# Channel attention with a gated MLP: six of eight f groups in seven products, two sums of each by transfers

## Chip, cores and metric

One Trainium2 chip, one core. The metric is the time of one execution on the device in microseconds; the median of three runs stands for a kernel.

## The reference

Four batches of channel attention (a softmax over a 256 x 256 matrix), whose result goes through a two-layer MLP with a squared gate. All in float32.

```python
def _attn_ref(q, k, v, tau) -> np.ndarray:          # q, k, v: 4 x 6080 x 256
    qn = q / (np.linalg.norm(q, axis=1, keepdims=True) + 1e-06)
    kn = k / (np.linalg.norm(k, axis=1, keepdims=True) + 1e-06)
    s = kn.transpose(0, 2, 1) @ qn / tau
    s = s - s.max(-1, keepdims=True)
    a = np.exp(s)
    a /= a.sum(-1, keepdims=True) + 1e-09
    return (v @ a).astype(np.float32)

def _moe_ref(x, w_in, w_out) -> np.ndarray:          # x: 24320 x 256, d_ff 2048
    h = x @ w_in
    beta = 1.0
    neg = h <= -beta
    pos = h >= beta
    g = np.where(pos, h, np.where(neg, 0.0, (h + beta) ** 2 / (4.0 * beta)))
    return (g @ w_out).astype(np.float32)
```

## The kernel before

**What is computed on TensorE.** For each batch the 256 x 256 attention matrix is multiplied into `w_in` once (`make_W`, `make_W2`); the result is stored in DRAM and loaded again for each use (`load_W`, an SP transfer of 896 KB). After that a batch is two large products: h = v W and out = g `w_out`. Every float32 value is split into a high half, rounded for TensorE's fast format, and a low half, the difference. A product is three matmuls: high by high, high by low, low by high (`mm3`, line 651). A product on 496 columns is now and then done on 512 (`width`, line 98).

**Tiling.** A batch's 6080 tokens are six pairs of token blocks, of 512 columns in the first four pairs and 496 in the last two. The 2048 columns of f are eight groups of 256 (i = 0 to 7). A group is one batch b, pair k and i, 192 in all, numbered g. In each group h is a 2 x 2 block product, and `h_ops` does it in the seven products of Strassen's method in Winograd's form: 21 matmuls in place of 24. The gate follows on ScalarE and VectorE (`saturate`, `square`, `clamp`), then the halves (`halves_of`: the high half a copy on ScalarE or VectorE, line 994 or 995, the low half a subtraction on VectorE, line 996).

**The second product.** `o_ops` does a plain group: eight products of three matmuls, on four banks of PSUM (`O00` to `O11`) that add up over the eight groups of a pair. `o_forms` does a group in the seven-product form. For it, sums of the four blocks of g are needed: `left` and `right` are two buffers with two blocks each, and `plus` (line 1059, its instruction at 1061) adds block to block on VectorE, three times in a group, while `added` (1080, its instruction at 1082) adds the fourth sum by a transfer between SBUF tiles, issued from GpSimd. Sums of the blocks of `w_out` (`S1` to `S4`) are made once by `make_forms` and stay in `wsum`. Groups in this form go in stacks, `STACKS = ((0,1),(4,5,6))`: within a pair, groups 0 and 1, then 4, 5 and 6. A stack's first two products are done group by group; the other five only when its last group is there, with copies and two sums of banks between them (lines 1101 to 1121: S2, then `add`, then S3, then `add`, then the last three). Before a stack begins and at the end of a pair the banks are emptied (`ends`): a ScalarE copy (line 1173), and a store, by SP, or by GpSimd with accumulation in DRAM for the pair's second half. The first pair has no stack; the last has `LAST = ((0,1),)`. So 22 pairs of five groups and one of two are in the form: 112 groups.

**What sets the order.** The whole program is written first as a list of operations with their reads and writes (`od.op`); `ORDER` is a table with the number of the next operation at each place, and `place` puts the operations in that order and gives each its buffers: 22 blocks (`NB`), 12 small ones (`NH`), 4 large ones for pairs of halves (`NX`), 3 for W (`NW`). Each engine, SP's and GpSimd's queue too, works its part off in order, and waits where an operand or a buffer isn't free. Numbers such as `T_FORM`, `due` and `pad` are used where the table is made; in the finished program the table decides.

## Time and profile before

| | before |
|---|---|
| median of three runs | 2098.42 us (2096.66 to 2106.02) |
| profiled execution, its own time | 2101.45 us |
| its span | 2099.5 us |
| TensorE busy | 2081.7 us, 9593 matmuls |
| VectorE busy | 2020.1 us |
| ScalarE busy | 1902.4 us |
| GpSimd busy | 265.0 us |
| DMA | 422.27 MB, mean 201 GB/s |

Busy time is the time in which at least one instruction of an engine is under way; consecutive instructions overlap a little, so an instruction's own duration is longer than the pace at which a row of them goes. The span runs from the first to the last instruction of the profiled execution. A transfer has two times: its issue on the engine whose queue it is in, and its landing.

### The profile page before, as it was taken

How to read it: one execution, taken by the hardware profiler on the slowest of the kernel's cores; microseconds unless marked ns; L12 is line 12 of the kernel's file. 1: busy time of each engine (PE TensorE's matmuls, PEld its weight loads, DVE VectorE, ACT ScalarE, POOL GpSimd, SP SyncE). 2: the span in 40 equal slices, each digit the busy share in tenths (PEclk: the TensorE clock that was granted, in tenths of full speed). 3: DMA queues.
4: the chain of work that ended last, by engine and by line, in shares of the span. 5: the costliest groups of instructions: out<-in, count | busy, mean ns of one | idle time of the engine just before them, and what ended most of it. 6: DMA issues, size and time to landing. Idle time of an engine off the chain costs nothing. (4 is left out here: it accounts for less than half of the span.)

```text
span 2099.5 us, 28487 instructions
## 1 busy us (share of the span) xinstructions
PE 2081.7 (99%) x9593; PEld 1741.5 (83%) x9593; DVE 2020.1 (96%) x3162; ACT 1902.4 (91%) x3111; POOL 265.0 (13%) x304
## 2 busy tenths in 40 slices
PE   9999999999999999999999999999999999999999
PEld 8888878888888888888788888888888888888887
DVE  7999999999999999999999999999999999999996
ACT  6899999999899999998899999989999999888884
POOL 0000011121101111111111120110111211111100
PEclk9999999999999999999999999999999999999999
DMA  9756667886668686785866887776786766566652
GB/s 381 283 206 201 214 173 228 227 236 163 162 215 264 175 251 201 214 256 140 204 171 205 253 212 245 207 197 200 194 214 180 169 184 162 148 176 170 164 132 69
DMA packets 133619, 422.27 MB, mean 201 GB/s; under 512 B 15202, under 2 KB 37346, under 8 KB 131170
## 3 DMA queue, kind: packets, MB, share of 16 engines
q1 hardware_dynamic: 91426, 344.70, 47.4%
q0 software_dynamic: 42048, 75.77, 22.8%
q8 instruction: 75, 1.23, 0.2%
q14 instruction: 70, 0.57, 0.1%
HBM read 310.05 MB, written 81.30 MB: 186 GB/s over the span
## 5 line engine op out<-in xcount | busy, mean ns | idle before, releaser
L654 PE MATMUL bank<-blk,w_mem 128*128 128x512 f32 (+1 forms) x4032 | 1038.3, 389 | 9.2 <-ACT bank L1016 5.4
L654 PEld LDWEIGHTS bank<-blk,w_mem 128*128 128x128 f32 x4032 | 749.9, 188 | 167.7 <-ACT bank L1016 8.9
L654 PE MATMUL bank<-x,wout 128*128 128x512 f32 (+1 forms) x2595 | 665.8, 387 | 1.6 <-DVE x L996 1.6
L654 PEld LDWEIGHTS bank<-x,wout 128*128 128x128 f32 x2595 | 485.7, 188 | 98.7 <-DVE x L996 2.4
L996 DVE TENSOR_TENSOR x<-blk,x 128x1024 fp32r<-128x1024 f32 (+1 forms) x384 | 459.9, 1210 | 6.4 <-ACT x L994 5.5
L978 ACT ACTIVATE blk<-blk 128x512 f32<-128x512 f32 (+3 forms) x576 | 438.0, 772 | 7.3
L983 DVE SCALAR_TENSOR_TENSOR blk<-bank,blk 128x512 f32<-128x512 f32 (+1 forms) x576 | 387.8, 681 | 15.3 <-ACT blk L978 14.1
L973 ACT ACTIVATE blk<-bank 128x512 f32<-128x512 f32 (+1 forms) x576 | 337.6, 593 | 46.7 <-PE bank L654 43.3
L994 ACT CAST x<-blk 128x1024 fp32r<-128x1024 f32 (+1 forms) x331 | 340.5, 1041 | 25.6 <-PE bank L654 10.4
L996 DVE TENSOR_TENSOR blk<-blk,blk 128x512 fp32r<-128x512 f32 (+1 forms) x336 | 226.7, 682 | 1.6
L1082 POOL DMA_DIRECT2D blk<-blk x112 | 98.5, 889 | 967.9 <-DVE blk L996 407.8
L654 PE MATMUL bank<-blk,wsum 128*128 128x512 f32 (+1 forms) x672 | 178.3, 387 | 0.0
L654 PE MATMUL bank<-x,wsum 128*128 128x512 f32 (+1 forms) x672 | 173.1, 388 | 0.0
L919 POOL DMA_DIRECT2D half<-vT x92 | 93.0, 1044 | 590.0 <-DVE blk L883 321.2
L994 ACT CAST blk<-blk 128x512 fp32r<-128x512 f32 (+1 forms) x242 | 148.3, 616 | 11.6 <-DVE blk L1061 8.9
L1061 DVE TENSOR_TENSOR blk<-blk,blk 128x512 f32<-128x512 f32 (+1 forms) x224 | 152.2, 682 | 1.8
L654 PEld LDWEIGHTS bank<-x,wsum 128*128 128x128 f32 x672 | 125.7, 188 | 25.8 <-DVE bank L1102 0.6
L654 PEld LDWEIGHTS bank<-blk,wsum 128*128 128x128 f32 x672 | 125.7, 188 | 24.9
L1019 DVE SCALAR_TENSOR_TENSOR bank<-bank,half 128x512 f32<-128x512 f32 (+1 forms) x192 | 132.7, 691 | 8.5 <-PE bank L654 2.4
L1023 DVE SCALAR_TENSOR_TENSOR half<-bank,half 128x512 f32<-128x512 f32 (+1 forms) x192 | 130.9, 682 | 5.5 <-PE bank L654 4.4
L654 PE MATMUL bank<-blk,blk 128*128 128x256 f32 (+2 forms) x704 | 135.4, 305 | 0.0
L973 ACT ACTIVATE blk<-half 128x512 f32<-128x512 f32 (+1 forms) x192 | 120.7, 629 | 11.8 <-DVE half L1023 10.2
(99 smaller groups left out, 2127.1 us busy)
## 6 DMA issues: line engine op xcount, KB each, us to landing
w_mem<-w_d SPq DMA_DIRECT2D x160, 896.0 KB, 6.0
blk<-kqT SPq DMA_DIRECT2D x60, 512.0 KB, 7.1
w_d<-w_mem SPq DMA_DIRECT2D x32, 896.0 KB, 7.8
blk<-kq SPq DMA_DIRECT2D x55, 512.0 KB, 6.2
half<-vT SPq DMA_DIRECT2D x75, 256.0 KB, 5.3
blk<-blk POOLq DMA_DIRECT2D x75, 256.0 KB, 5.2
kq<-kq SPq DMA_DIRECT2D x18, 1024.0 KB, 9.1
outT<-half SPq DMA_DIRECT2D x64, 256.0 KB, 6.1
```

The source lines that it names most:

```text
L654: nc.tensor.matmul(out, lhsT=lhs(a), rhs=rhs(c), start=start and m == 0, stop=stop and m == 2, skip_group_check=skip)
L919: op("POOL", POOL_DMA, lambda: nc.gpsimd.dma_start(out=tt(x), in_=blk(j, h), accum_op=ALU.add), w=[ts[x]], due=due + d, gates=gates, size= ...
L973: op("ACT", act_ps(n) if psum else act_us(n), lambda: nc.scalar.activation(pb.ap[:, j, :n], src(), AF.Relu, bias=0.5, scale=0.5), r=[h, pb ...
L978: op("ACT", act_us(len(us) * n), lambda: nc.scalar.activation(at(), at(), AF.Square), r=[pb], w=us, due=due, tag=(53, due - G * (due // G)))
L983: op("DVE", dve_us(n), lambda: nc.vector.scalar_tensor_tensor(out=us(), in0=src(), scalar=1.0, in1=us(), op0=ALU.max, op1=ALU.min), r=[h, ...
L994: op("ACT", act_us(m * n), lambda: nc.scalar.copy(half_(0), src()), r=r, w=[t], due=d_hi, other=("DVE", dve1_us(m * n), lambda: nc.vector. ...
L996: op("DVE", dve_us(m * n), lambda: nc.vector.tensor_tensor(out=half_(1), in0=src(), in1=f32(half_(0)), op=ALU.subtract), r=r, w=[t], due=d ...
L1019: op("DVE", dve_us(n), lambda: nc.vector.scalar_tensor_tensor(out=bb.ap[:, :n], in0=z.ap[:, :n], scalar=-1.0, in1=m5.ap[:, :n], op0=ALU.mu ...
L1023: op("DVE", dve_us(n), lambda: nc.vector.scalar_tensor_tensor(out=h22.ap[:, :n], in0=z.ap[:, :n], scalar=-1.0, in1=m5.ap[:, :n], op0=ALU.m ...
L1061: op("DVE", dve_us(n), lambda: V.tensor_tensor(out=at(out), in0=at(a), in1=at(c), op=ALU.add), r=[b for p, j in (a, c) for b in (p[0], p[1 ...
L1082: op("POOL", POOL_DMA, lambda: nc.gpsimd.dma_start(out=at(out), in_=at(a), accum_op=ALU.add), r=[a[0][0], a[0][1 + a[1]], out[0][0]], w=[o ...
```

## The change

`STACKS` and `LAST` both become `((0,1,2),(4,5,6))`, so six groups of every pair but the first are in the seven-product form, 138 in all; groups 3 and 7 stay plain. The sum of `right`'s two blocks is made by `added` in place of `plus`, so a group has two transfers and two VectorE sums. One more set of forms (i = 2) is made. The form `S4` goes into the place of `w_out`'s block (x = 0, ct = 1), which a group in the seven-product form doesn't read, once the first pair, whose groups are plain, has read it; `wsum` has three forms in place of four, and there is one more small buffer (`NH` 13). In the last pair the first half's results are copied to SBUF and kept there (`kept`), and VectorE adds the second half's to them before the store; before, that pair's banks were emptied at its end alone. `ORDER` is a new table.

```diff
--- before.py
+++ after.py
@@ -251,7 +251,7 @@
 G = 16
 U = 32
 NB = 22
-NH = 12
+NH = 13
 NX = 4
 NW = 3
 
@@ -269,153 +269,160 @@
 T_SO = 2.7
 T_P4 = -5.7
 ORDER = (
-    "c-n2c4@`3XmnU{P&mD%PH;ls?>pIpLYmIS@wT30cI4mVBWhrG@$6*M=I)pMTVW~?ULRd<yF|2hgF@!jdYh2c$gdv7yD9iF=UBXh<CDyu*wZ^*E"
...
+    "c-mdM4NQ7}mnU{P-ao^`bBD(gV~lGYW2`mCSmUzRSi&00G7LjmhVZZ~!!is*DPycP##m#GHP%?;IK;S?Sk@BCQii$=!$TQ{r7TMb!??y8*BWDt"
...
 )
-STACKS = ((0,1),(4,5,6))
-LAST = ((0,1),)
-FORMED = (0,1,4,5,6)
+STACKS = ((0,1,2),(4,5,6))
+LAST = ((0,1,2),(4,5,6))
+FORMED = (0,1,4,2,5,6)
 STARTUP = (
     ('v', 0, -463.4, 13),
     ('out', 0, -426.7, 16),
@@ -534,7 +541,7 @@
     kq_early = Pool(kq_mem, kq_all)
     pools["g"].held[:4] = [kq_all] * 4
     for i in FORMED:
-        pools[f"wsum{i}"] = Pool([sb(f"wsum{i}", [2, 4, P], F32R)])
+        pools[f"wsum{i}"] = Pool([sb(f"wsum{i}", [2, 3, P], F32R)])
     win_dram = [dram.tile([P, 2 * WIN], U32, name=f"win_d{i}") for i in range(FP // 2)]
     row_dram = [dram.tile([CT, P], F32, name=f"row_d{b}") for b in range(B)]
     w_dram = [[dram.tile([P, WSZ], U32, name=f"w_d{b}_{i}") for i in range(FP)] for b in range(B)]
@@ -596,12 +603,13 @@
         convert(w_out[i].rearrange("p a f -> p (a f)"), wout_buf[i], lambda: wout_buf[i].ap, due, gates)
 
     form_buf = {i: buf(f"wsum{i}") for i in FORMED}
-    FORMS = (S1, S2, S3, S4)
+    FORMS = (S1, S2, S3)
+    a21_buf = {i: Buf(ap=wout[:, i]) for i in FORMED}
 
     def wform(i, s, a):
         if s in FORMS:
             return form_buf[i].ap[:, a, FORMS.index(s), :]
-        x, ct = {A11: (0, 0), A12: (1, 0), A22: (1, 1)}[s]
+        x, ct = {A11: (0, 0), S4: (0, 1), A12: (1, 0), A22: (1, 1)}[s]
         return wout[:, i, a, x, ct * P:(ct + 1) * P]
 
     def make_forms(i, due, step=0.4):
@@ -612,13 +620,19 @@
         op("DVE", dve_us(512), lambda: nc.vector.tensor_tensor(out=w_ap(), in0=flat(0), in1=flat(1), op=ALU.add),
            r=[wout_buf[i], pb], w=[w], due=due, tag=11)
         at = {A11: 0, A21: 1, A12: 2, A22: 3}
-        forms(lambda x: f_ap()[:, FORMS.index(x) * P:(FORMS.index(x) + 1) * P],
+        forms(lambda x: f_ap()[:, (S1, S2, S3, S4).index(x) * P:][:, :P],
               lambda x: w_ap()[:, at[x] * P:(at[x] + 1) * P], [w, pb], f, due + step)
         fl = lambda a: to.ap[:, a].rearrange("p j f -> p (j f)")
-        op("ACT", act_us(512), lambda: nc.scalar.copy(fl(0), f_ap()), r=[f, pb], w=[to],
+        late = lambda a: wout[:, i, a, 0, P:2 * P]
+        part, last = (lambda: f_ap()[:, :3 * P]), (lambda: f_ap()[:, 3 * P:])
+        op("ACT", act_us(384), lambda: nc.scalar.copy(fl(0), part()), r=[f, pb], w=[to],
            due=due + 2 * step, tag=12)
-        op("DVE", dve_us(512), lambda: nc.vector.tensor_tensor(out=fl(1), in0=f_ap(), in1=fl(0).bitcast(F32),
+        op("DVE", dve_us(384), lambda: nc.vector.tensor_tensor(out=fl(1), in0=part(), in1=fl(0).bitcast(F32),
                                                               op=ALU.subtract), r=[f, pb], w=[to], due=due + 3 * step, tag=13)
+        op("ACT", act_us(128), lambda: nc.scalar.copy(late(0), last()), r=[f, pb], w=[a21_buf[i]],
+           due=due + 2 * step, tag=12)
+        op("DVE", dve_us(128), lambda: nc.vector.tensor_tensor(out=late(1), in0=last(), in1=late(0).bitcast(F32),
+                                                              op=ALU.subtract), r=[f, pb], w=[a21_buf[i]], due=due + 3 * step, tag=13)
 
     def forms(out, src, r, w, due):
 
@@ -946,7 +960,7 @@
     NG = len(groups)
     mark = [None] * (NG + 8)
     o_buf, out_buf = {}, {}
-    gt, gu = {}, {}
+    gt, gu, kept = {}, {}, {}
 
     def stack_of(g):
 
@@ -1075,18 +1089,18 @@
                 m = od.width(n, TB, j in (V_T3, V_22, V_T4, V_21))
                 mm3(out.ap[:, :m], lambda a: wform(x, s, a), lambda c: at(c, m), start, False)
 
-            op("PE", mm_us(n), fn, r=[t, wout_buf[x], form_buf[x]], w=[out], due=due, tag=(63, s))
+            op("PE", mm_us(n), fn, r=[t, wout_buf[x], form_buf[x], a21_buf[x]], w=[out], due=due, tag=(63, s))
 
         def added(out, a, c, due):
             at = lambda x: x[0][0].ap[:, x[1], :n]
             op("POOL", POOL_DMA, lambda: nc.gpsimd.dma_start(out=at(out), in_=at(a), accum_op=ALU.add),
-               r=[a[0][0], a[0][1 + a[1]], out[0][0]], w=[out[0][1 + out[1]]], due=due - 8, size=n * 512, tag=(62, "d"))
+               r=[a[0][0], a[0][1 + a[1]], out[0][0]], w=[out[0][1 + out[1]]], due=due - 8, size=n * 512, pad=3.0, tag=(62, "d"))
 
         f = d + T_FORM
         halves(left, (V_11,), f + 18, 0)
         plus((left, 0), (right, 0), (left, 0), f + 18.5)
         halves(left, (V_T1,), f + 19, 1)
-        plus((right, 0), (right, 1), (right, 0), f + 20.5)
+        added((right, 0), (right, 1), (right, 0), f + 20.5)
         plus((left, 0), (right, 1), (left, 0), f + 20)
         halves(left, (V_T2,), f + 20.5, 2)
         halves(right, (V_T3, V_22), f + 22, 1)
@@ -1133,11 +1147,11 @@
                 o = o_buf[b, k, y, ct]
                 c0 = b * N + t0 + y * n
 
-                def store(yb, m0, m1, due, ct=ct, c0=c0):
+                def store(yb, m0, m1, due, w=None, ct=ct, c0=c0):
                     to = outT[ct * P:(ct + 1) * P, c0 + m0:c0 + m1]
                     if g < FP or g >= NG - FP or i < STACKS[1][0]:
                         out_buf[c0, ct] = Buf(ap=outT)
-                        op("SP", 0.45, lambda: nc.sync.dma_start(out=to, in_=yb.ap[:, :m1 - m0]), r=[yb],
+                        op("SP", 0.45, lambda: nc.sync.dma_start(out=to, in_=yb.ap[:, m0 if w else 0:m1 if w else m1 - m0]), r=[yb, *([w] if w else ())],
                            w=[out_buf[c0, ct]], due=due, size=(m1 - m0) * 512, tag=67)
                     else:
                         op("POOL", POOL_DMA, lambda: nc.gpsimd.dma_start(out=to, in_=yb.ap[:, :m1 - m0], accum_op=ALU.add),
@@ -1152,27 +1166,38 @@
                         mm3(o.ap[:, :m], lambda a: wout[:, i, a, x, ct * P:(ct + 1) * P], lambda c: at(c, m),
                             g == 0 and x == 0, ends(g) and (x == 1 or end))
 
-                    op("PE", mm_us(n), fn, r=[t, wout_buf[i]], w=[o], due=d + T_O + dues[2 * ct + x], tag=(69, y, x, ct))
+                    op("PE", mm_us(n), fn, r=[t, wout_buf[i], *([a21_buf[i]] if i in FORMED and (x, ct) == (0, 1) else ())], w=[o], due=d + T_O + dues[2 * ct + x], tag=(69, y, x, ct))
                 due = d + dues[2 * ct + 1] + 3
                 if end:
 
                     (t, at), m = gt[g, 1, y], n // 2
                     for m0, m1, bank in ((0, m, "A"), (m, n, "B")):
-                        yb, q = buf("y"), buf(bank)
-                        op("ACT", act_us(m1 - m0), lambda yb=yb, m0=m0, m1=m1: nc.scalar.copy(
-                            yb.ap[:, :m1 - m0], o.ap[:, m0:m1]), r=[o], w=[yb], due=due, tag=70)
+                        (yb, ws), q = kept[y, ct], buf(bank)
+                        w = ws[m0 > 0]
+                        op("DVE", dve_us(m1 - m0), lambda yb=yb, m0=m0, m1=m1: nc.vector.tensor_tensor(
+                            out=yb.ap[:, m0:m1], in0=o.ap[:, m0:m1], in1=yb.ap[:, m0:m1], op=ALU.add), r=[o, yb], w=[w],
+                           due=due, psum=True, tag=70)
                         op("PE", mm_us(m1 - m0), lambda q=q, m0=m0, m1=m1: mm3(
                             q.ap[:, :m1 - m0], lambda a: wout[:, i, a, 1, ct * P:(ct + 1) * P],
                             lambda c: at(c, n)[:, m0:m1], True, True), r=[t, wout_buf[i]], w=[q], due=due, tag=71)
-                        op("DVE", dve_us(m1 - m0), lambda yb=yb, q=q, m=m1 - m0: nc.vector.tensor_tensor(
-                            out=yb.ap[:, :m], in0=q.ap[:, :m], in1=yb.ap[:, :m], op=ALU.add), r=[q], w=[yb],
+                        op("DVE", dve_us(m1 - m0), lambda yb=yb, q=q, m0=m0, m1=m1: nc.vector.tensor_tensor(
+                            out=yb.ap[:, m0:m1], in0=q.ap[:, :m1 - m0], in1=yb.ap[:, m0:m1], op=ALU.add), r=[q, yb], w=[w],
                            due=due + 1, psum=True, tag=72)
-                        store(yb, m0, m1, due + 1)
+                        store(yb, m0, m1, due + 1, w)
+                elif g == len(groups) - 1:
+                    yb, (w, _) = kept[y, ct]
+                    op("DVE", dve_us(n), lambda o=o, yb=yb: nc.vector.tensor_tensor(
+                        out=yb.ap[:, :n], in0=o.ap[:, :n], in1=yb.ap[:, :n], op=ALU.add), r=[o, yb], w=[w],
+                       due=due, psum=True, tag=75)
+                    store(yb, 0, n, due + 1, w)
                 elif ends(g):
                     yb = buf("y")
                     op("ACT", act_ps(n), lambda o=o, yb=yb: nc.scalar.copy(yb.ap[:, :n], o.ap[:, :n]), r=[o], w=[yb],
                        due=due, tag=73)
-                    store(yb, 0, n, due + 1)
+                    if g < NG - FP:
+                        store(yb, 0, n, due + 1)
+                    else:
+                        kept[y, ct] = yb, [Buf(ap=False) for _ in range(2)]
```

Three places show how the new order differs. The first is VectorE in the last pair but one of the second batch, group 6 of its fifth pair, where the blocks are clamped and summed (`blk_20_8143` is its right, `blk_16_7853` its left buffer before; `blk_10_7794` and `blk_16_8144` in the change). Before:

```order
L983 SCALAR_TENSOR_TENSOR blk_20_8143<-bank_97,blk_20_8143 128x496
L983 SCALAR_TENSOR_TENSOR blk_20_8143<-half_86,blk_20_8143 128x496
L1061 TENSOR_TENSOR blk_16_7853<-blk_20_8143,blk_16_7853 128x496
L1061 TENSOR_TENSOR blk_18_8019<-blk_18_8019 128x496
L737 TENSOR_SCALAR cols_94<-cols_94,tau_sb 128x2
L1061 TENSOR_TENSOR blk_20_8143<-blk_20_8143 128x496
L1019 SCALAR_TENSOR_TENSOR bank_97<-bank_103,half_93 128x496
L996 TENSOR_TENSOR blk_15_7122<-blk_12_7695,blk_15_7122 128x496
L996 TENSOR_TENSOR blk_17_8359<-blk_16_7853,blk_17_8359 128x496
L1061 TENSOR_TENSOR blk_16_7853<-blk_20_8143,blk_16_7853 128x496
```

The change:

```order
L997 SCALAR_TENSOR_TENSOR blk_10_7794<-bank_98,blk_10_7794 128x496
L897 TENSOR_TENSOR blk_15_8286<-half_87,blk_15_8286 128x512
L1075 TENSOR_TENSOR blk_16_8144<-blk_10_7794,blk_16_8144 128x496
L997 SCALAR_TENSOR_TENSOR blk_10_7794<-half_91,blk_10_7794 128x496
L1010 TENSOR_TENSOR blk_13_7326<-blk_12_8232,blk_13_7326 128x496
L1009 CAST blk_15_7288<-blk_16_8144 128x496
L1010 TENSOR_TENSOR blk_15_7288<-blk_16_8144,blk_15_7288 128x496
L1033 SCALAR_TENSOR_TENSOR bank_98<-bank_104,half_83 128x496
L897 TENSOR_TENSOR blk_15_8243<-half_92,blk_15_8243 128x512
L1075 TENSOR_TENSOR blk_16_8144<-blk_10_7794,blk_16_8144 128x496
```

Before, three sums of that group stand here, the middle one with the right buffer alone; in the change the two with both buffers stand, and the right buffer's own sum is in GpSimd's queue.

The second place is ScalarE in the same group, from the rounding of the left buffer ahead of the transfer (a `CAST` to one row) to the one that needs the transfer's result (a `CAST` to `x`, two rows). Before:

```order
L994 CAST blk_19_8192<-blk_16_7853 128x496
L978 ACTIVATE blk_14_8357<-blk_14_8357 128x496
L1110 COPY half_93<-bank_101 128x496
L880 CAST blk_15_7105<-half_87 128x512
...
L973 ACTIVATE blk_14_8464<-bank_96 128x496
L978 ACTIVATE blk_14_8464<-blk_14_8464 128x496
L994 CAST x_765<-blk_14_8422 128x2x496
L994 CAST x_844<-blk_14_8357 128x2x496
L994 CAST x_731<-blk_16_7853 128x2x496
```

The change:

```order
L1008 CAST blk_13_8248<-blk_16_8144 128x496
L1121 COPY bank_99<-bank_100 128x496
L1008 CAST x_805<-blk_16_7618 128x2x496
L1124 COPY half_90<-bank_102 128x496
...
L987 ACTIVATE blk_22_8511<-bank_103 128x496
L987 ACTIVATE blk_16_8579<-bank_97 128x496
L992 ACTIVATE blk_16_8579<-blk_16_8579 128x496
L992 ACTIVATE blk_22_8511<-blk_22_8511 128x496
L1008 CAST x_805<-blk_16_8144 128x2x496
```

Between the two roundings of the left buffer stand 17 instructions before and 25 in the change.

The third place is TensorE at the end of the program (the banks `O00` to `O11` are `bank_98` to `bank_101` before and `bank_99` to `bank_102` in the change). Before:

```order
L654 MATMUL bank_101<-x_731,wout 128x496 x3
L654 MATMUL bank_98<-x_844,wout 128x496 x3
L654 MATMUL bank_100<-x_839,wout 128x496 x3
L654 MATMUL bank_98<-x_844,wout 128x496 x3
L654 MATMUL bank_100<-x_839,wout 128x496 x3
L654 MATMUL bank_100<-x_731,wout 128x512 x6
L654 MATMUL bank_100<-x_765,wout 128x496 x6
L654 MATMUL bank_101<-x_731,wout 128x496 x3
L654 MATMUL bank_101<-x_765,wout 128x496 x6
```

The change:

```order
L668 MATMUL bank_101<-x_729,wout 128x512 x3
L668 MATMUL bank_99<-x_805,wout 128x496 x3
L668 MATMUL bank_100<-x_710,wout 128x496 x3
L668 MATMUL bank_100<-x_805,wout 128x496 x3
L668 MATMUL bank_102<-x_729,wout 128x512 x3
L668 MATMUL bank_101<-x_729,wout 128x512 x3
L668 MATMUL bank_101<-x_729,wout 128x496 x3
L668 MATMUL bank_102<-x_729,wout 128x496 x3
L668 MATMUL bank_100<-x_710,wout 128x496 x3
L668 MATMUL bank_100<-x_807,wout 128x496 x3
L668 MATMUL bank_99<-x_710,wout 128x496 x3
L668 MATMUL bank_99<-x_807,wout 128x496 x6
```

Before, the program closes with products of plain groups alone; in the change the last products of the stack 4, 5, 6 and those of the plain group 7 stand among each other.

## Rows read from the trace of the kernel before

**Rows 1.** The page's first part: busy us, share of the span, instructions.

```profile
PE 2081.7 (99%) x9593; PEld 1741.5 (83%) x9593; DVE 2020.1 (96%) x3162; ACT 1902.4 (91%) x3111; POOL 265.0 (13%) x304
```

**Rows 2.** Stretches: length, PE, PEld, DVE, ACT, POOL busy, clock, DMA share, GB/s.

```profile
0.00:87.50 87.50, 84.62 (x401) 73.29 (x402) 73.60 (x136) 63.84 (x91) 3.35 (x10) 0.98 0.91 353
...
612.50:700.00 87.50, 87.50 (x421) 73.48 (x420) 86.65 (x133) 85.49 (x139) 14.72 (x17) 1.00 0.85 263
962.50:1050.00 87.50, 82.82 (x383) 69.78 (x382) 82.29 (x131) 76.00 (x130) 11.86 (x13) 1.00 0.73 177
...
1662.50:1750.00 87.50, 87.50 (x387) 72.21 (x386) 86.69 (x129) 82.19 (x135) 9.98 (x12) 1.00 0.68 176
2012.50:2100.00 87.50, 82.88 (x377) 69.79 (x375) 65.47 (x94) 53.15 (x86) 7.30 (x8) 0.99 0.36 93
```

**Rows 3.** Waits of TensorE: for whom, us in total, times, longest us.

```profile
PE bank L654 <- ACT bank L1016: 5.4, 3, 3.2
PE bank L654 <- DVE bank L1019: 1.8, 2, 1.0
PE bank L654 <- DVE x L996: 1.6, 2, 1.2
...
PE bank L654 <- DVE bank L1102: 1.2, 1, 1.2
...
PE bank L654 <- DVE half L1023: 0.5, 1, 0.5
```

**Rows 4.** The chain of waits: start us, us, what.

```profile
1643.62 232.00 PE bank L654 x1020
...
1900.08 1.20 DVE blk L983 x2
...
1965.07 130.32 PE bank L654 x587
```

**Rows 5.** Groups by line and form: busy us, mean ns; line 1061: min/median/max ns.

```profile
L994 ACT CAST blk<-blk 128x512 fp32r<-128x512 f32 x166 | 102.5, 621 | 8.0 <-DVE blk L1061 7.4 <-DVE blk L983 0.3
L995 DVE CAST blk<-blk 128x512 fp32r<-128x512 f32 x59 | 25.2, 429 | 1.4 <-PE bank L654 0.5 <-ACT blk L702 0.3
...
L1061 DVE TENSOR_TENSOR blk<-blk x112: 664/684/700, 178.7 to 2027.8; 128x512 f32<-128x512 f32 x75, 128x496 f32<-128x496 f32 x37
```

**Rows 6.** Line 1082, the transfers: issue ns min/median/max, who waited, landing.

```profile
L1082 POOL DMA_DIRECT2D blk<-blk x112: 859/862/1264, 185.3 to 2033.3; - x112
...
  ACT x L994: 8.1, 4
  DVE x L995: 3.0, 2
...
DMA to landing us min/median/max: 3.2/4.8/13.5
```

**Rows 7.** Timeline from 1002 to 1019 us: start us, us, engine, instruction [idle before].

```profile
1002.20 0.87 POOL L1082 DMA_DIRECT2D blk<-blk  x1 [2.36 <-PE bank L654]
...
1002.92 0.39 SPq L745 DMA_DIRECT2D row_d<-cols  x1
1003.39 0.42 SPq L555 DMA_DIRECT2D w_mem<-w_d  x1
...
1009.76 1.94 ACT L994 CAST x<-blk 128x992 fp32r<-128x992 f32 x2
1015.78 1.02 ACT L994 CAST x<-blk 128x992 fp32r<-128x992 f32 x1 [4.07 <-DMA blk<-blk]
...
1017.67 0.57 ACT L1016 COPY bank<-bank 128x496 f32<-128x496 f32 x1
...
1018.30 1.65 PE L654 MATMUL bank<-blk,w_mem 128*128 128x512 f32 x6 [3.21 <-ACT bank L1016]
```

**Rows 8.** Timeline of TensorE at 1965 us.

```profile
1965.07 0.72 PE L654 MATMUL bank<-x,wout 128*128 128x496 f32 x2 [1.16 <-DVE x L996]
```

**Rows 9.** DMA queues: packets, MB, share of 16 engines' span.

```profile
q1 hardware_dynamic: 91426, 344.70, 47.4%
q0 software_dynamic: 42048, 75.77, 22.8%
```

More of the change, by code (lines that the diff above doesn't have):

```diff
@@ new lines @@
+    "&)IwZ60Q%J0F24TnD|->1;Mi@X25WC_G;!@Fu}h7Km`DReaN%@<PX6UI$kTG!m-lhSOy*4dl~e<-0svPAE*cw_RXZ!32_;&B<j7**gZ_%Z8gYu"
+    "AuG?xqX2i47>1Ws0Kq;bKxAMpVuYmT^sYa;3Z~wNoV4F%k!5A^w~**!WfZ=8<%2JyQ2SUvhtpV0SQi31pz;Q%Cu;shO`p#n=_@6_%*lgst!*65"
+    "ghY*n)4F#ZN@t_`y(L$uhMA*tIl&NIN43uIVQpQxVD&$3S(~Yq%)-K?VmS%7`w+7zCs&TP4TjbGiFdzF6atW!HhSf%bl5Ml!ddJZ;4l~xX|LUl"
+    "jR)M~$e+J@Ets#j)Ln`>HCl-212#RxR`R*8YiK~<7t|9`WyF%0$;Q#MM$!@s8gQdPA2+FE73kYs?$zKk{U6((4(&T!c|eReZ2oA{>CwluW}OiF"
+    "+;OS>cF%ld?TPv1)`IS+fa21uqFa+vC9!E3gx95Rs6$8(e3k875Gf}uf#<E{`jEh)OX|jq5!1^4lC%B`4`fx5nTM@4xNq9QxE6G7IRd|N0RDSJ"
@@ new lines @@
+    "Y;1ZP%@yYJ^<CI(>b9TEyF2?Jea0K*8a^itPZ?fzRz-!PbVIC#P5VysV7mM9LyjAkKyAHw9=%D*^xo}24Jpaz&nkHsdt4eqBa*2`P}dt&qj=KL"
+    "os*z^!&fQ-!w=(!9uU==!g`EvtU0u%P}=8IHtfyV<vt1l088ErszfkW!&37m^h_W$1iMq4%}lfZL*VJL&Rz}<TpurO>`$lRG^*@d#y>^7%cA5_"
+    "VR)e4RHZR!_Kaup%5(EPRI>Us)N~mL25?b4=)XVHYT`PBy(vfEN)x)C74g14v^!O{g0-BPH`zRk{*=~&gq$bEGiONJt#xTYKXPMx+Yue0E)X7S"
+    "8i?fBJReA}-XW<_)un>T<}nIBUs0A&ixPT>3s)yU!a4F)(sP8i6WCCJC%kkVjSR{CrBUq2dAf>D>bDR18wSb7fj8B&`{G_*FC|5SWTEn$j%KFr"
+    "K6?~s=JT_3Q=NnvVO|G<hM;j6#gisD?K74<-Ik;`GyiIxk|ak8gT@s!b?0mfbfJVHVE3OYinfOM?)ZAFalC!)jlRtqoV~e(_+1!Vxf(N!73W|0"
@@ L419 @@
+    "ZS<ublRR=pGqn4_1pEDqj*=+Rfl)-;!D#{0j$U3z&$9J6O)nh{4h~ef!3kbRQ<W_+@Y=Of9!Ko#m%loNSo;Hy;E<ZD(6<yn@bGp`q}~4IwR@*X"
+    "2NwLKjX*H;z=az9wJ7deDji=h;M@g4ews$p+NMdDT*!0=?aW(=4n<8+%^I#@&&fBO_mgLdp9rm=WEq_xh#)^jUaH&8n2-KyQM<!|bht77-K$QS"
+    "OQ&4zBkoLRhz>>k{{c=a8vO"
+)
+STACKS = ((0,1,2),(4,5,6))
+LAST = ((0,1,2),(4,5,6))
+FORMED = (0,1,4,2,5,6)
 STARTUP = (
```

278 lines of the change are left out of this document (136 added, 142 removed).

## The prediction

> **What bounds the kernel now.** I read the busy shares first, then the table of stretches, the waits of TensorE, the chain of waits, and last the lines of the transfers. TensorE is busy for 2081.7 of 2099.5 us, VectorE for 2020.1, ScalarE for 1902.4, GpSimd for 265.0 [rows 1]. The granted clock is 1.00 in every stretch shown but the first and last [rows 2], so the 2.4 GHz level holds and no clock is to be won. TensorE's 17.8 us of idle time lie at the start (2.9 us in the first 87.5), at the end (4.6) and in one stretch around 1000 us (4.7); two stretches between have none [rows 2]. A busy TensorE here is one at its pace: the chain has 1020 matmuls in 232.00 us, mostly of 512 columns, 0.2275 us each, and 587 in 130.32 us, mostly of 496, 0.222 us each [rows 4]. So time is won by taking matmuls away, as long as the two engines that feed them keep up. VectorE is close behind: of its 79.4 us of idle time, 13.9 lie in the first stretch and 22.0 in the last [rows 2], which leaves 43.5 us for the 1925 us between, 2.3%.
>
> **Matmuls removed.** Groups in the seven-product form go from 112 (22 pairs of five and one of two) to 138 (23 pairs of six). Each of the 26 new ones needs 7 products of 3 matmuls in place of 8, so 78 matmuls go. The order of the program has that many fewer, 75 of them at 496 columns and 3 at 512, since the kernel mixes the widths: 75 x 0.222 + 3 x 0.2275 = **17.3 us** off TensorE [rows 4]. All of it is on the path now.
>
> **VectorE.** The sum of the two right halves (the `blk<-blk` of line 1061, 112 of them [rows 5]) becomes a transfer. Each new group adds two sums and three more subtractions for low halves: 26 x 5 = 130. Net 18 more instructions of this kind. One lasts 0.684 us by itself [rows 5], but back to back two take 1.20 us on the chain [rows 4], so 0.60 each: 18 x 0.60 = 10.8. The sixth set of forms, the split of the forms' rounding into 384 and 128 columns, the closing sums of the last pair and a few copies that change engine come to about 5 more (some ten instructions at 0.6 or less). Together **+16 us**, to 2036. Against 2082 us of TensorE that is 97.8%, where it is 96.2% now. None of it lies on the path as long as the order keeps VectorE ahead, which is the main doubt and a rival below.
>
> **ScalarE.** 57 more roundings of one row (0.62 us alone, about 0.51 back to back, since two double ones take 1.94 at 1009.76) and ten more double ones (0.95): about +42 us [rows 5, 7], to 1945 or 93% of the new span. Covered by idle time that it has.
>
> **Transfers.** 276 instead of 112. Issuing one takes GpSimd 0.862 us [rows 6], so it grows by 141 us to about 406, a fifth of the span: not a limit. In the DMA engines, the software queue took 22.8% of the span for 75.77 MB [rows 9], 6.3 us for a MB; 164 more at about 0.26 MB are 42.5 MB, so 13% of the span more on top of 70%. The one stretch that has 0.85 today would come near 0.98. There TensorE lost nothing at 0.85 [rows 2]; nothing in the trace of before shows what 0.98 does in the middle of the kernel, while the first stretch, full of loads, has 0.91.
>
> What a transfer costs is lateness. One lands 4.8 us after its issue in the median, 3.2 at best, 13.5 at worst, and those who use it waited 8.1 + 3.0 us in all, six times [rows 6]. The worst shows how it reaches TensorE: issued at 1002.20 beside the store of the norms' row and a load of weights, landed at 1015.7, ScalarE stood 4.07 us before the rounding that needs it, the copy of a bank behind that came late, and TensorE waited 3.21 us [rows 7]. A second cost 1.16 us at 1965 [rows 8]. So 4.4 us of TensorE's idle time are late transfers. The new order gives them more room: at the very place of the worst one, 17 instructions stand on ScalarE between the rounding ahead of the transfer and the one behind it before, and 25 after; over all transfers, in the order in which the program is written, 16 products of three matmuls stand between a transfer's last producer and its first user in the median before (8 at the least) and 22 after (13 at the least), which at 0.68 us each is 11 us (5) and 15 us (9). Twice the transfers with 4 us more room: I take back 2 of the 4.4 us. The bounds are all 4.4 regained, and 6.4 more lost, which is 4.4 / 112 for each of the 164 new ones (a landing time as now, and no room gained).
>
> The Trainium skill ("SBUF — State Buffer", the section on SBUF's two separate sides) has a rule against such a change: descriptors of a transfer issued from GpSimd are not written while VectorE runs a copy in its two-port mode, and such a transfer took 3.1 us where alone it took 0.62. Here the longest issue is 1.264 us against 0.862 in the median [rows 6], a delay of 0.4 us, about one such copy (0.429 us [rows 5]); by the row the rule costs 0.4 us of 9 us of room, and by the page's figure 2.5 us, which would still be inside.
>
> **Denser VectorE.** Waits of TensorE put down to VectorE in the steady part are 1.8 + 1.6 + 1.2 + 0.5 = 5.1 us, and 1.16 of it is the late transfer above [rows 3, 8]. With 16 us more work in 17 us less time its idle time between first and last stretch falls from 43.5 to about 10. If waits grew as idle time shrinks, 4 us would become 16. But busy time counts the 0.08 us by which each instruction overlaps the next [rows 4, 5], so that part of the idle time is hidden, and the order was drawn up for the new load: I take **+3 us**, bounds 0 and +13.
>
> **Start and end.** The last pair had only its first two groups in the form, so that plain products closed it; now a group of three is finished there, and its four later products wait for two VectorE sums of 0.68 us with one or two products ahead (0.66 us each), and the last sum runs on VectorE instead of a ScalarE copy. In the last stretch VectorE is busy for 65.5 of 87.5 us [rows 2], so it has room. I take **+1 us**, bounds 0 and +3. The start is left as it is, and GpSimd's queue, SyncE's loads and the stores of the last pair (half of them now stay in SBUF until a sum is added) are off the path.
>
> **Sum.** Against the profiled execution (2101.45 us, span 2099.5): -17.3 - 2 + 3 + 1 = -15.3, so 2086.1. The median of the runs shown is 3.0 below that execution, so the forecast is **2083 us**, 0.73% faster. Its own range is 2078 to 2088.
>
> **Rivals.**
> VectorE sets the end. Its idle time today could be waits it can't shed (for ScalarE, for banks). If all 79.4 us stay, the span is 2020 + 16 + 79 = 2115, the median **2114**, slower by 0.8%. It decides from the point where VectorE's idle time can't fall below 46 us (2082 - 2036), 36 of which the first and last stretch hold. If half of the fall is had, 2098. For it: 2.3% idle between the ends. Against it: TensorE had no idle time at all in stretches where VectorE was busy for 86.7 of 87.5 us [rows 2], 99%, more than the 97.8% that is asked for on average. Chance 0.13, half of it with a slower kernel.
>
> Transfers come late. The 6.4 us above in place of the 2 regained: 2083 + 8.4 = **2091**, within 0.5%. For it: the fuller DMA engines, three stores of the norms' row like the one at 1002.92, and GpSimd's queue in order, where a transfer that waits for VectorE holds back those behind it. Against it: the room. Chance 0.16.
>
> The new order waits less than the old. Late transfers gone and nothing new: -17.3 - 4.4, **2076 or 2077**. Chance 0.14.
>
> The change not doing what it says is no case: the order has the 78 fewer matmuls.
>
> **Chances.** Forecast 0.55, the rivals 0.13, 0.16 and 0.14, and 0.02 for the rest. Faster by over 0.5% (below 2087.9, about what a measurement of this kernel can tell from no change): 0.52 of the forecast's 0.55 and 0.14, so 0.66. Slower by over 0.5%: 0.07. The rest, 0.27, within. For 8 in 10 the range takes the forecast, the late transfers and half of the gain beyond, with the milder part of VectorE's case: 2075 to 2097.
>
> **What would show it.** TensorE at 99% busy with 78 fewer matmuls and idle time of 15 to 22 us bears out the step that carries the sum. VectorE's busy share near 97.5% with no wait of TensorE on it over 2 us bears out the third term; VectorE at 96% and TensorE's idle time above 35 us would show the first rival. The users of the transfers should wait less than today's 11 us in all, at a landing of 5 to 7 us in the median; waits of 20 us and more, followed by waits for the copy of a bank, would show the second. The forecast is wrong if waits of TensorE grow by over 8 us wherever they come from.

## Result and the profile after

| | before | after |
|---|---|---|
| median of four runs each | 2100.82 us (2096.66 to 2106.02) | 2076.6 us (2076.11 to 2077.91) |
| profiled execution, span | 2099.5 us | 2074.8 us |
| TensorE busy, idle | 2081.7, 17.8 us | 2063.2, 11.6 us |

The ratio is 0.9884 (95%: 0.9859 to 0.9910), 1.2% faster. The forecast was 2083, 6 us above the result, which lies below the forecast's own range (2078 to 2088), at the bottom of the wide one (2075 to 2097), and at the very number of the rival "the new order waits less". The gain is further off than the time: 15.3 us were forecast, and 24.7 came by the spans (24.2 by the medians). The forecast was counted from a median of three runs that lies 2.4 us below that of four.

Part 1 of the page of after answers to [rows 1]:

```profile
PE 2063.2 (99%) x9515; PEld 1725.5 (83%) x9515; DVE 2025.3 (98%) x3203; ACT 1935.6 (93%) x3193; POOL 412.2 (20%) x468
```

The 78 matmuls are gone. GpSimd (412) and ScalarE (1936) come near what was forecast (406 and 1945). VectorE has 41 instructions more and is busy for only 5 us more, not 16.

Stretches of after (length, busy time of the five engines, clock, DMA share, GB/s), against [rows 2]:

```profile
0.00:87.50 87.50, 86.19 (x418) 75.28 (x419) 73.00 (x136) 65.74 (x93) 3.03 (x10) 1.00 0.90 340
612.50:700.00 87.50, 87.49 (x408) 72.96 (x407) 86.92 (x132) 87.06 (x142) 19.42 (x22) 1.00 0.94 257
962.50:1050.00 87.50, 87.50 (x408) 74.13 (x407) 85.73 (x144) 82.66 (x144) 19.12 (x22) 1.00 0.79 202
1987.30:2074.80 87.50, 82.05 (x370) 68.36 (x368) 79.51 (x119) 61.66 (x100) 16.20 (x18) 1.00 0.58 129
```

The stretch around 1000 us, which lost 4.7 us, loses none. A DMA share of 0.94 in the second row costs TensorE nothing. In the last stretch VectorE now works for 79.5 us, where it had 65.5.

Waits of TensorE in after (for whom, us in total, times, longest), against [rows 3]:

```profile
PE bank L668 <- ACT bank L1030: 1.9, 5, 0.7
PE bank L668 <- DMA blk<-win_d: 1.1, 1, 1.1
...
PE bank L668 <- DMA w_mem<-w_d: 0.7, 1, 0.7
PE bank L668 <- DVE blk L1010: 0.6, 1, 0.6
PE bank L668 <- DVE bank L1116: 0.5, 2, 0.3
PE bank L668 <- DVE x L1010: 0.5, 2, 0.2
```

No stop is longer than 1.1 us. Those put down to VectorE in the steady part fell from 5.1 to 1.6 us, those to ScalarE's copies of banks from 5.4 to 1.9. The view of the transfers names nobody who waited for one; their issue and landing times, against [rows 6]:

```profile
L1096 POOL DMA_DIRECT2D blk<-blk x276: 859/862/1855, 181.5 to 2053.7; - x138
...
DMA to landing us min/median/max: 3.2/4.9/11.2
```

In the median they land as late as before (4.8 us), and the order has room for it. By the signs that the prediction named, TensorE idles for 11.6 us, less than the 15 to 22 that were to bear out its sum; VectorE is busy for 97.6% with no wait of TensorE on it over 0.6 us; and nobody waits for a transfer.

The 24.7 us of the span split at the first matmul of h and the last matmul of all: 3.1 at the start (that matmul comes at 67.74 us, before at 70.89), 22.2 between, and 0.6 lost behind the last matmul (4.8 us to the end, before 4.1).

### The profile page after: what moved, and what is told of

It reads as the page before. It is cut to its first block, busy times and chain, and to the rows that moved or that the text cites. A ratio compares the mean times of both kernels' runs of the same rounds, so it can differ in the third digit from the quotient of the medians.

```text
span 2074.8 us, 29131 instructions
## 1 busy us (share of the span) xinstructions
PE 2063.2 (99%) x9515; PEld 1725.5 (83%) x9515; DVE 2025.3 (98%) x3203; ACT 1935.6 (93%) x3193; POOL 412.2 (20%) x468
## 4 chain that ended last, share of the span: by engine, by line
PE 80%; DVE 7%; ACT 2%; DMA 2%; issue 1%; POOL 0%; SPq 0%; DVEq 0%; ACTq 0%; POOLq 0%
PE bank L668 80%; DVE blk L997 2%; DVE x L1010 1%; DMA outT<-half 1%; DVE blk L1010 1%; DVE blk L1075 1%; DVE blk L681 0%; DMA w_mem<-w_d 0%; DVE half L1037 0%; DVE bank L1033 0%; ACT blk L987 0%; ACT x L1008 0%; ACT blk L992 0%; DMA blk<-win_d 0%; DVE bank L1116 0%
## 5 line engine op out<-in xcount | busy, mean ns | idle before, releaser
L668 PE MATMUL bank<-x,wout 128*128 128x512 f32 (+1 forms) x2541 | 655.3, 387 | 0.2 <-DVE x L1010 0.2
L1096 POOL DMA_DIRECT2D blk<-blk x276 | 249.9, 935 | 1266.2 <-DVE blk L1010 295.9
L1008 ACT CAST x<-blk 128x1024 fp32r<-128x1024 f32 (+1 forms) x341 | 350.9, 1042 | 2.2 <-PE bank L668 1.9
L1010 DVE TENSOR_TENSOR blk<-blk,blk 128x512 fp32r<-128x512 f32 (+1 forms) x414 | 276.2, 676 | 2.9 <-ACT blk L1008 1.8
L668 PE MATMUL bank<-blk,wsum 128*128 128x512 f32 (+1 forms) x828 | 218.6, 388 | 0.6 <-DVE blk L1010 0.6
L1008 ACT CAST blk<-blk 128x512 fp32r<-128x512 f32 (+1 forms) x299 | 181.8, 616 | 6.9 <-DVE blk L1075 4.4
L1075 DVE TENSOR_TENSOR blk<-blk,blk 128x512 f32<-128x512 f32 (+1 forms) x276 | 185.2, 676 | 1.0
L668 PEld LDWEIGHTS bank<-blk,wsum 128*128 128x128 f32 x828 | 154.8, 188 | 32.0 <-DVE blk L1010 1.2
L997 DVE SCALAR_TENSOR_TENSOR blk<-half,blk 128x512 f32<-128x512 f32 (+1 forms) x192 | 129.7, 676 | 0.0
L1028 ACT COPY half<-bank 128x512 f32<-128x512 f32 (+1 forms) x192 | 111.8, 582 | 18.7 <-PE bank L668 16.9
```

Source lines behind the costliest of these rows:

```text
L668: nc.tensor.matmul(out, lhsT=lhs(a), rhs=rhs(c), start=start and m == 0, stop=stop and m == 2, skip_group_check=skip)
L997: op("DVE", dve_us(n), lambda: nc.vector.scalar_tensor_tensor(out=us(), in0=src(), scalar=1.0, in1=us(), op0=ALU.max, op1=ALU.min), r=[h, ...
L1008: op("ACT", act_us(m * n), lambda: nc.scalar.copy(half_(0), src()), r=r, w=[t], due=d_hi, other=("DVE", dve1_us(m * n), lambda: nc.vector. ...
L1010: op("DVE", dve_us(m * n), lambda: nc.vector.tensor_tensor(out=half_(1), in0=src(), in1=f32(half_(0)), op=ALU.subtract), r=r, w=[t], due=d ...
L1028: op("ACT", act_ps(n), lambda: nc.scalar.copy(m5.ap[:, :n], a.ap[:, :n]), r=[a], w=[m5], due=d - U, tag=58)
L1075: op("DVE", dve_us(n), lambda: V.tensor_tensor(out=at(out), in0=at(a), in1=at(c), op=ALU.add), r=[b for p, j in (a, c) for b in (p[0], p[1 ...
```

## Experiments

Ratios are to the kernel before on the same chip (0.1% is 2.1 us). The runs are spread over four chips. The changed kernel itself was run again on one of them, with a ratio of 0.9872; its variants with small transfers and with sums back on VectorE ran on another chip and are held against it by their ratios.

**Matmuls taken out of the order before.** In both runs an early return ahead of the product leaves it out:

```diff
 def fn(o=o, at=at, x=x, ct=ct):        # second run: y=y too
+    if g >= FP and (y, ct, x) == (0, 0, 0) and (i == 2 or i == 3 and 1 <= k <= 3 and b == 1):
+        return
```

> The kernel before with its order as it is, and 78 matmuls left out: the first of the products in 26 groups that are in the plain form (so those groups' outputs lack one product; VectorE, ScalarE and the transfers keep all their work). My theory, that TensorE's time sets the length and the matmuls are worth their full 0.222 us each: 17.3 us less than before, and TensorE's idle time stays at 17 to 19 us. The rival, that part of the gain of the change is hidden behind VectorE and came from elsewhere: less than 12 us off, and TensorE's idle time grows by over 5 us.

Its `y` was read only when the order was laid out, when it is 0 for both halves, so 156 matmuls were left out (9437 remain), some 35 us of them. Measured: 2101.09 against 2104.85, ratio 0.9978 (0.9967 to 0.9989): 4.6 us of 35. The mended run:

> The kernel before with its order as it is and 78 matmuls left out: one product of each of 26 plain groups (those groups' outputs lack it). It mends the first run, whose edit left out two products in each, 156 matmuls, 34.6 us of TensorE's time: there VectorE and ScalarE, with unchanged work, may have become the bound by going twice too far. If 78 matmuls are worth their 17.3 us in the order before as they are in the new one: 17.3 less than before (14 to 18). If the order before has no room behind TensorE, as the 3.8 us for 156 matmuls suggest: under 6 us less, with the new waits of TensorE for banks (lines 1016 and 1019) in every pair.

Measured: 2100.24 against 2103.01, ratio 0.9989 (0.9979 to 0.9999): **2.3 us (0.2 to 4.4) for 78 matmuls**, not 17.3. Part 1, waits of TensorE, and two groups of instructions (busy us, mean ns, idle before) of this run; of before and after the same two groups:

```profile
PE 2074.3 (99%) x9515; PEld 1723.3 (82%) x9515; DVE 2018.6 (96%) x3162; ACT 1900.8 (91%) x3111; POOL 264.8 (13%) x304
PE bank L654 <- ACT bank L1016: 6.0, 9, 2.7
PE bank L654 <- DVE bank L1019: 2.4, 5, 1.0
L654 PE MATMUL bank<-blk,w_mem 128*128 128x512 f32 (+1 forms) x4032 | 1043.8, 390 | 10.5 <-ACT bank L1016 6.0
L654 PEld LDWEIGHTS bank<-blk,w_mem 128*128 128x128 f32 x4032 | 747.9, 188 | 179.8 <-ACT bank L1016 14.9
```

```profile
L654 PE MATMUL bank<-blk,w_mem 128*128 128x512 f32 (+1 forms) x4032 | 1038.3, 389 | 9.2 <-ACT bank L1016 5.4
L654 PEld LDWEIGHTS bank<-blk,w_mem 128*128 128x128 f32 x4032 | 749.9, 188 | 167.7 <-ACT bank L1016 8.9
```

```profile
L668 PE MATMUL bank<-blk,w_mem 128*128 128x512 f32 (+1 forms) x4032 | 1032.9, 389 | 2.8 <-ACT bank L1030 1.9
L668 PEld LDWEIGHTS bank<-blk,w_mem 128*128 128x128 f32 x4032 | 749.7, 188 | 161.3 <-ACT bank L1030 5.9
```

TensorE is busy for 7.4 us less, not 17.3: the same 4032 matmuls of h, none of which was touched, take 5.5 us longer in all (some 1.7 of it in a stretch of half clock at 1018 us), and their weight loads stand idle for 12 us more, 6 of it for ScalarE's copies of banks. So part of the wait stands inside "busy". A matmul lasts 0.39 us by its record, and a row of them goes at 0.2275 us each [rows 4], so a start that is up to some 0.16 us late leaves no idle time. Counted from start to start (what exceeds 0.225 us while the matmul before is still under way, from 75 us on), 17 us of TensorE's busy time in this run are such delay, and 7 in before. That is why the chain's long unbroken pieces before [rows 4] didn't show how near the next wait was.

**Is it VectorE's work that eats it?** One of VectorE's sums cut down in the order before, alone and with the first run's edit:

```diff
-        def plus(out, a, c, due):
-            at = lambda x: x[0][0].ap[:, x[1], :n]
+        def plus(out, a, c, due, m=n):
+            at = lambda x: x[0][0].ap[:, x[1], :m]
...
-        plus((right, 0), (right, 1), (right, 0), f + 20.5)
+        plus((right, 0), (right, 1), (right, 0), f + 20.5, 16)
```

> The kernel before with the 112 sums of the right halves on VectorE shrunk from 496 or 512 columns to 16 (the sum is left out in the other columns): some 60 us less work on VectorE, all matmuls kept. By the prediction's view, that VectorE keeps TensorE waiting for some 3 to 5 us: 3 to 5 us less than before. The rival, that VectorE holds TensorE up by more than the named waits show: 8 us less or more.

> The kernel before with both: 78 matmuls left out in 26 plain groups, and the 112 sums of the right halves at 16 columns. With the matmuls alone left out the time fell by 3.8 us only, not 17.3. If VectorE's work is what ate the rest: 17.3 us less than the kernel with the light sums alone (16 to 18.5). The rival, that the fixed order (the banks' turns, ScalarE) holds TensorE back wherever a product is taken out, whatever VectorE has to do: under 10 us less than it.

Measured: 0.9980 (0.9966 to 0.9994) alone, 0.9961 (0.9947 to 0.9975) with both; the second holds 156 fewer matmuls too, by the slip told above. With VectorE at 1972 us, 119 us idle, 156 matmuls are worth 4 us more. So it isn't the amount of VectorE's work. Waits of TensorE and of VectorE in the run with both:

```profile
PE bank L654 <- ACT bank L1016: 9.2, 14, 1.7
PE bank L654 <- DVE bank L1019: 3.9, 8, 1.0
DVE blk L983 <- ACT blk L978: 25.0, 57, 1.4
```

VectorE, with time to spare, waits 25 us for ScalarE's squares (line 978) ahead of its own clamps (983), where it waited 14.1 before, and TensorE waits for ScalarE's copies of banks (1016). Each engine takes its instructions in a fixed order and gets its data from the other two; the rival's fixed order is what the number fits, which is an argument and no test of it. Whether less work on ScalarE would set it free wasn't tried.

**The same 78 in the new order.**

```diff
                 mm3(out.ap[:, :m], lambda a: wform(x, s, a), lambda c: at(c, m), start, False)
+                if j == V_T2 and (x == 2 or h >= NG - FP and x >= 4):
+                    mm3(out.ap[:, :m], lambda a: wform(x, s, a), lambda c: at(c, m), False, False)
```

> The changed kernel with 78 matmuls more: in each of its 26 new groups in the seven-product form one product is done twice (so those groups' outputs are off), at the same place in the order; all else stays. If TensorE's time sets the length of the changed kernel: 17.3 us more than the changed kernel, less its few waits that the extra work fills, 14 to 17.5. The rival, that in the changed kernel VectorE sets the pace and TensorE waits for it as soon as it is faster: under 10 us more.

> The changed kernel itself, on the chip of the runs beside it, as their zero: 24 us less than before, as measured. VectorE's mean time for a sum of two 512-column tiles was 0.687 us in the trace of before and 0.682 in that of after: if that is the chip's or the execution's and not the kernel's, it comes out nearer to the other kernels of this chip.

Measured: 2092.63, ratio 0.9949 (0.9935 to 0.9963), and 2076.08, ratio 0.9872 (0.9856 to 0.9888). **In the new order the 78 are worth 16.6 us**, and with as many matmuls as before the change still gives 10.7 (7.8 to 13.7). TensorE is busy for 2080.2 of 2090.6 us there, and the delay inside its busy time is 7 us, as in after, so its time sets the length. Putting matmuls in and leaving them out aren't mirror images, though: whether 78 more in the order before would cost 17 us too, or 78 fewer in the new one would give less, wasn't tried. Nor was a new table for the kernel before with all its matmuls, which could hold a part of the 10.7.

A 512-column sum of VectorE's took 0.682 us in the mended run above and 0.684 in this zero, so the 0.687 in the trace of before was the execution's, not the kernel's.

**Late transfers.** In the kernel before and in the changed one alike:

```diff
         def added(out, a, c, due):
-            at = lambda x: x[0][0].ap[:, x[1], :n]
+            at = lambda x: x[0][0].ap[:, x[1], :16]
```

> The kernel before, with each of the 112 transfers between tiles moving 16 columns instead of 496 or 512 (the sum of the right halves is left out in the other columns); the order and the number of transfers stay. If late transfers cost 4.4 us of TensorE's idle time before, as the prediction put it: the stops of 3.21 us at 1002 to 1019 us and of 1.16 us at 1965 are gone, and the time is 4.4 us less. The rival, that the store of the norms' row and its queue make them late whatever they move: the stop of about 3 us at 1019 us stays, and the time is within 1 us of before.

> The changed kernel with each of its 276 transfers moving 16 columns instead of 496 or 512 (the sums made by transfers are left out in the other columns). If no transfer is late any more, as its waits say: within 1 us of the changed kernel. The rival, that the fuller DMA engines (the share is 0.94 in one stretch) hold up loads or roundings somewhere: 2 us less or more.

Measured: 2094.38 against 2104.85, ratio 0.9959 (0.9944 to 0.9975), **8.6 us (5.3 to 11.8)**; and in the changed kernel 2074.45, ratio 0.9869 (0.9853 to 0.9885), not told apart from 0.9872. Waits of TensorE in the first:

```profile
PE bank L654 <- DVE bank L1019: 1.8, 2, 1.0
...
PE bank L654 <- DVE half L1023: 0.5, 1, 0.5
PE bank L654 <- DVE x L996: 0.5, 1, 0.5
PE bank L654 <- ACT bank L1016: 0.3, 1, 0.3
```

The wait for copies of banks, 5.4 us before, is gone all but 0.3, as are 1.1 of the 1.6 of line 996 [rows 3]: late transfers stood behind up to 6.2 us of named waits, where I had counted the 4.4 of two stops. (Up to: one of these waits, 1.7 us at 278 us, is also missing from the run with the edit at the start, whose transfers are whole.) The rest of the 8.6 can lie inside busy time, where the delay fell from 7 to 5 us, and in what follows a stop (the last section).

**The start.** Two pieces of the next batch are set ahead of the norms' sums in the table as it is read:

```diff
...
+        sums = next(j for j, (m, _) in enumerate(moved) if self.ops[m].tag[0] == 82)
+        later = [j for j, (m, _) in enumerate(moved) if j > sums and self.ops[m].tag[0] == 74][:2]
+        early = [moved[j] for j in later]
+        for j in reversed(later):
+            del moved[j]
+        moved[sums:sums] = early
...
```

> The kernel before with two pieces of the next batch's products set ahead of the norms' sums in TensorE's order at the start; all else as it is. In the trace of before TensorE waits 1.58 us for VectorE just ahead of those sums, and the granted clock is at half for the next 3.4 us. My theory of the 3.2 us that the changed kernel gains ahead of its first h matmul: the wait goes and with it the half clock, the first h matmul comes about 3.2 us earlier, the time is about 3 us less. The rival, that VectorE's chain of sums sets the start: the wait comes back behind the two pieces or in the next one, and the time is within 1 us of before.

Measured: 2100.27, ratio 0.9983 (0.9971 to 0.9994), 3.6 us (1.3 to 6.1). By the trace the first matmul of h comes at 69.50, 1.4 us earlier, not 3.2. Timelines of TensorE at the start, before, with this edit, and after (start, length, instruction, idle before):

```profile
49.13 1.05 PE L1223 MATMUL bank<-ones,blk 128*128 128x1 f32 x8 [1.58 <-DVE blk L1241]
50.04 5.39 PE L1202 MATMUL bank<-kq 96*128 96x256 f32 x16
```

```profile
49.39 1.04 PE L1232 MATMUL bank<-ones,blk 128*128 128x1 f32 x8
50.30 1.97 PE L1211 MATMUL bank<-kq 128*128 128x256 f32 x8
53.28 0.71 PE L726 MATMUL bank<-half,ones 128*128 128x128 f32 x4 [1.01 <-DVE half L719]
```

```profile
47.83 0.95 PE L1248 MATMUL bank<-ones,blk 128*128 128x1 f32 x8
48.65 3.70 PE L1227 MATMUL bank<-kq 128*128 128x256 f32 x16
```

The wait came back one step further, 1.01 us in place of 1.58, as the rival said; the half clock did not (8 matmuls in 1.97 us, 16 in 5.39 before), and the time fell by what my theory said and not by under 1 us. The mean granted clock of the 12 runs is 0.999, against 0.998 in the 23 of before. So neither holds whole. In after VectorE's last sum of squares itself starts earlier, at 45.24 in place of 48.38, and TensorE doesn't wait for it: 22 conversions of weights stood on VectorE ahead of that sum before (lines 572 to 585), and 11 stand there now.

**Three together**, with the first run's edit (so 156 matmuls here too):

> The kernel before with the three edits together: 78 matmuls left out in 26 plain groups, transfers of 16 columns, and two pieces ahead of the norms' sums at the start (outputs lack one product in 26 groups and most of the right halves' sums). If the gain of the changed kernel is the sum of these three and nothing else: 17.3 + 4.4 + 3.2 = 24.9 us less than before, TensorE's idle time near 12 us as in the changed kernel. The rival, that these overlap (one wait taking the place of another), and the new order itself brings the rest: 20 us less or fewer.

Measured: 2088.39 against 2104.85, ratio 0.9927 (0.9912 to 0.9943), 15.4 us. The transfers and the start alone add up to 8.6 + 3.6 = 12.2, so the 156 matmuls are worth some 3 us here as well. The order before doesn't come near the new one by these edits.

**VectorE's price in the new order.** The right halves' sum back on VectorE, in all groups and in a third of them:

```diff
-        added((right, 0), (right, 1), (right, 0), f + 20.5)
+        (plus if True else added)((right, 0), (right, 1), (right, 0), f + 20.5)   # the other run: if i in (1, 5)
```

> The changed kernel with the sum of the right halves back on VectorE in all 138 groups, at the place in the order where the transfer was issued; the other 138 transfers stay. VectorE gets 138 x 0.60 = 83 us more, 2025 + 83 = 2108 us. If VectorE sets the end as soon as its work passes TensorE's 2063 us, with the idle time of its first and last stretch (about 36 us) on top: about 2145 us, TensorE idle for some 70 to 80 us. The rival, that the order has room and VectorE's busy time overstates its work (each of its instructions overlaps the next by 0.08 us): 2085 us or less.

> The changed kernel with the sum of the right halves back on VectorE in two groups of six (46 of 138), the rest by transfer. VectorE gets 46 x 0.60 = 28 us more, 2053 us beside TensorE's 2063. By the way I priced VectorE's density (waits grow as its idle time between the first and last stretch shrinks, and here it would be gone): 10 to 25 us more than the changed kernel. The rival, that VectorE costs nothing until its work passes TensorE's: within 3 us of the changed kernel.

Measured, in all groups, 2143.99, ratio 1.0202 (1.0186 to 1.0219), and in a third, 2098.03, ratio 0.9979 (0.9968 to 0.9989). Part 1 of both pages, and of the first a stretch and a group:

```profile
PE 2103.6 (98%) x9515; PEld 1715.4 (80%) x9515; DVE 2104.4 (98%) x3341; ACT 1943.9 (91%) x3193; POOL 290.4 (14%) x330
267.76:357.02 89.26, 88.05 (x389) 70.03 (x388) 88.80 (x138) 83.23 (x139) 12.51 (x14) 1.00 0.69 199
L668 PE MATMUL bank<-blk,w_mem 128*128 128x512 f32 (+1 forms) x4032 | 1054.1, 393 | 27.6 <-DVE bank L1033 11.7
```

```profile
PE 2076.0 (99%) x9515; PEld 1721.4 (82%) x9515; DVE 2049.6 (98%) x3249; ACT 1939.0 (93%) x3193; POOL 371.5 (18%) x422
```

By their ratios the two runs lie 69 and 22 us above the changed kernel, by the spans of the executions shown 67.3 and 17.4, for 79.1 and 24.3 us more work on VectorE: 0.7 to 0.9 us for each. TensorE has almost the same to do. Its 9515 matmuls are the same, but where the kernel expects TensorE to wait, `width` does some of them on 512 columns in place of 496: 411 more in the first run and 216 in the second, at 0.0055 us each [rows 4] 2.3 and 1.2 us. In the stretch shown VectorE is busy for 99.5%. TensorE reads 98% busy in the first run, 40 us more than in after: most of that is waiting, since the delay inside busy time, counted as above, is 41 us there, 17 in the second run and 7 in after. VectorE's idle time was 49.5 us in after, 37.7 and 42.6 here. The sums stand where the transfers were issued; an order drawn up for them wasn't tried.

## Why the prediction was right, and where it wasn't

The time lies in the wide range, and partly by luck: the term that carries the sum held in the new order, the others missed, most of them to the same side, and the low starting point took back 2.4 us of it.

**Matmuls removed** (-17.3): the size holds in the new order, 16.6 us. The step "all of it is on the path now" doesn't: in the order before the same 78 gave 2.3 us. The premise behind it, that a busy TensorE is one at its pace, was read from the chain's long pieces [rows 4] and from stretches without idle time [rows 2], and these can't show how near the next wait is. The gain needs the order made anew as much as the seven products.

**Transfers** (-2): mis-sized. The places of the order were read rightly (25 instructions in place of 17), and the upper bound of the gain, all of it back, is what came; but the stake was 8.6 us, not 4.4, since only the two stops whose chain was followed were counted. The fuller DMA engines cost nothing measurable.

The longest issue is now 1.855 us, 1.0 over the median, against 0.4 before; nobody waited for it. It isn't the delay that the prediction weighed: it is the last of four issues in a row on GpSimd, and VectorE runs no copy beside it. From the timeline of after:

```profile
765.08 0.86 POOL L1096 DMA_DIRECT2D blk<-blk  x1 [5.00 <-PE bank L668]
765.62 1.22 POOL L1157 DMA_DIRECT2D outT<-half  x1
766.17 1.57 POOL L933 DMA_DIRECT2D half<-vT  x1
766.77 1.85 POOL L1096 DMA_DIRECT2D blk<-blk  x1
```

In after, sixteen issues over 0.9 us have a copy or conversion of VectorE beside them and no other issue just ahead; the longest of these takes 1.357 us, 0.5 over the median. The Trainium skill ("SBUF — State Buffer", the section on SBUF's two separate sides) gives 3.1 us for a transfer that overlaps such a copy and 0.62 for one alone, by estimate a delay of 2.5 us. No issue in the traces before and after has as much, and the rule decides nothing here.

**Start** (0): wrong, 3.1 us by the trace, 1.7 of it a stretch of half clock that the execution shown of before had (last section). "The start is left as it is" held for the source text; the table had moved 11 conversions on VectorE behind the sums that TensorE waits for.

**Clock** ("no clock is to be won", so 0): wrong. The execution that was read had one short stretch at half, but most runs of the kernel before have more, and some 5 us of the gain go with them (last section).

**VectorE** (+16 us of work; +3 of waits): its busy time grew by 5, or by 7 between two executions in which an instruction takes the same (2018.6 us in the mended run, 2025.7 in the zero). Busy time hides the rest: VectorE works in 279 stretches without a gap in the changed kernel and in 372 in the kernel before, and each counts once the 0.08 us by which an instruction outlasts the start of the next. By this estimate 7 us of work don't show, and about 14 of the 16 are there. The 0.60 us for a sum was read from two clamps [rows 4]; the 138 sums put back cost 0.57 each (79.1 us). The waits put down to VectorE fell by 3.5 us. What density itself costs isn't settled: of the 10.7 us that remain with equal matmuls, 8.6 are transfers and 3.1 the start, less 0.6 at the end, which leaves a loss of 0.4 us with an uncertainty of some 4, so +3 is neither shown nor excluded. These parts overlap, too: some 4 of the 10.7 go with the clock, which stands in the start's 3.1 and may stand in the 8.6 (its mean is 0.9998 in those five runs and 0.9981 in the 20 of before beside them, and 0.001 goes with about 2.5 us by the medians of the last section).

**End** (+1): 0.6 by the trace. Of the 4.6 us that the prediction read as idle at the end, 0.5 lie beyond the span.

**Rivals.** "The new order waits less" came true in its number (2076 or 2077) and not in its sum: late transfers gave twice the 4.4, the start 3, and part of it was lost again elsewhere or lies within the uncertainty. "VectorE sets the end" didn't happen, but its mechanism is real and close. It was to decide where idle time can't fall below 46 us; the runs with more work put the floor at 38 to 43, and after has 49.5. So some 7 to 12 us of slack in idle time are left; by the traces the first 24 us of extra work used 7 of it and paid 17 in time. With the second sum left on VectorE this order stands at 2144, slower than before.

## What to carry to other kernels

In a program whose engines run in a planned order, take the price of removed work from putting it back in the new order and from leaving it out of the old one: here 16.6 and 2.3 us for 78 matmuls each, and neither is wrong. A bottleneck engine that reads 99% busy can hold tens of microseconds of waiting; look at the same instructions' summed time, at the idle time of its weight loads and at the time from one start to the next in two kernels before calling it at its pace. When a table of the order is new, compare every engine's rows at the start too, not only where the source changed. And look at the clock of every run, not of one execution, before putting it at nothing.
